# Refill order of the wide weight pieces, gate gathers one slot ahead, and five weight positions in a mixture-of-experts kernel

## The chip, the cores and the metric

The kernel runs on one core of a Trainium2 chip. The metric is the device time of one execution in microseconds; of several executions the median is given. A profiled execution has a time of its own and a span, which goes from its first to its last instruction.

## The reference

Two stages. The first is causal attention over 4 batches, 8 heads, 576 tokens of width 64, blended per head with a linear memory; its output, reshaped to 2304 tokens of width 512, is `x`. The second sends every token to one of 8 experts:

```python
logits = x @ w_gate
e_idx = np.argmax(logits, axis=1)
gate_w = probs[np.arange(N), e_idx]
eom = 1.0 / (1.0 + np.exp(-(x @ w_output_gate)))
for e in range(E):
    mask = e_idx == e
    if not mask.any():
        continue
    h = np.maximum(x[mask] @ w1[e], 0.0)
    ye = h @ w2[e]
    out[mask] = gate_w[mask, None] * eom[mask, e, None] * ye
```

`w1[e]` is 512 x 1024 and `w2[e]` 1024 x 512, both float32, so one expert's weights are 4 MB.

## The kernel before

The attention stage takes roughly the first 205 us and is not touched. Behind it, tokens are sorted by expert into blocks of up to 128 rows of one expert, called slots. One slot's work is done early for the expert with the most tokens (the "star" functions); 17 main slots (`NMAIN`) follow in a fixed loop; and remainders of experts that would fill only a small part of a slot are collected into two group tiles: four experts' remainders of up to 32 rows, then two of up to 64 rows.

**A main slot.** `gather(s)` fetches the 128 rows of `x` by an indirect DMA on POOL, `gather_gate(s)` the 128 gate factors by another. `stage_x` transposes the rows on PE (L1376), copies them out on ACT twice, as `xh` rounded and as `x32` full (L1381, L1383), and POOL takes the difference `xl` (L1384). `gemm1` is 24 products (L1405): each weight is split into a high part `whi` and a low part `wlo`, and the product is the sum of whi·xh, whi·xl and wlo·xh. ACT applies the ReLU (L1418). `stage_h` transposes the result (L1431), ACT copies it (`hT`, `hh`, L1434 and L1435) and POOL forms `hl` (L1436). `gemm2` is 24 more products, ACT scales the result by the gate factor (`y`, L1443) and POOL scatters it (`scatter`, L1459). The loop runs `gemm1` of slot s+1, then `stage_x` of slot s+2, then `gemm2` of slot s, with `stage_h` of slot s+1 in its middle.

**Expert weights.** The experts of the main slots stand in an order of "positions": position 0 is the star expert, and `NPOS` positions are loaded. `fetch` (L377, DMAs on SP, 512 KB each) fills four buffers `kept`, and `high`, `low`, `ready` (L1097 to L1104) split a piece on DVE: 0.7 us for a cast and 1.2 us for a subtraction, eight pieces to an expert. Only two positions fit into `whi` and `wlo`, so `load_expert(e)` (L1335) makes DVE wait, by `sem_1` and `sem_2`, until the slots of position e-2 have used its half. Before a slot PE waits on `sem_w` until its own position is split.

**Wide pieces.** The group tiles need weights of several experts at once. They run in 24 units, two to a slot in slots 2 to 13: unit (s, 0) before `gemm2(s)`, unit (s, 1) behind it (`plan`, `point`, `unit`, L1562). A unit reads one of two 1 MB buffers `wide`, which alternate. `wide_load(u)` (L1521) fills one with 2 or 4 DMAs issued by ACT, and PE waits on a semaphore for all of them (L1565). `refill(s, half)` (L1624) issues the load that uses the buffer that unit (s, half) has freed; it is read one slot later. ACT runs its instructions in the order in which they are written.

**Around slot 0.** `gather_gate(s)` for slots 0 to 3 and `star_out`, the scatter of the early slot, stand in a row on POOL; later gates are gathered by `gather(s + 4)`. `group_rows` (L1323) computes the rows of the group tiles. A scratch tile `hhs` (L1255) shares its memory (tag `hh`) with the tile `hh` of slot 0, and the star's result `ye` (L1358) shares the tag `xc` with the gathered rows of a group.

**The end.** Behind the loop every engine reads the number of slots and jumps over a branch (L1708, L1709) that would run 18 further slots one at a time; SP then waits for the last scatter.

The functions that are touched, with their lines:

Of the kernel before, what the change touches and what calls it, by code (L numbers as in the profile page):

```python
# [10 lines left out]
F32 = mybir.dt.float32  # L11
# [9 lines left out]
P = 128  # L21
# [3 lines left out]
DM = H * D  # L25
E = 8
F = 1024
# [5 lines left out]
KC = DG + P  # L33
QK = KC + S
NMAIN = 17
NPOS = 6
NREST = 18
NSLOT = NMAIN + NREST
NEND = E + 1
QUARTERS = 4  # L40
# [92 lines left out]
def attn_moe(ctx: ExitStack, tc: tile.TileContext, qk, vd, mz, mt, rz, beta, wgo, w1, w2, out):  # L133
# [49 lines left out]
    ze = {}  # L183
# [193 lines left out]
    def fetch(e, c):  # L377
        n = 8 * e + c
        if len(kept) < 4:
            kept.append(raw_tile(f"kept{n}"))  # L380
        raw = raws[e, c] = kept[n % 4]
        if c == 0:
            fetching["e"] = SY.value_load(order[0:1, e:e + 1], min_val=0, max_val=E - 1)
        send(raw, fetching["e"], c)
# [645 lines left out]
    def star_out():  # L1030
        V.scalar_tensor_tensor(jc, stars, 65536.0, jc, op0=ALU.mult, op1=ALU.add)
# [151 lines left out]
    def rows(i):  # L1183
        V.tensor_scalar(rowi[i], pps[i], float(MID), 0.0, op0=ALU.add, op1=ALU.add)
# [9 lines left out]
    def take():  # L1194
        d, ok, qc, qn, qt, hc, hn, ht, qr = (t8[n] for n in ("d", "ok", "qc", "qn", "qt", "hc", "hn", "ht", "qr"))
        V.scalar_tensor_tensor(d, sizes, -BIG, fin["nps"], op0=ALU.add, op1=ALU.subtract)
        V.scalar_tensor_tensor(qn, sizes, BIG, star, op0=ALU.is_le, op1=ALU.mult)
        V.scalar_tensor_tensor(ok, d, 64.0, qn, op0=ALU.is_lt, op1=ALU.subtract)
        V.tensor_scalar(ok, ok, 0.0, 0.0, op0=ALU.max, op1=ALU.add)
        V.scalar_tensor_tensor(qc, d, 32.0, ok, op0=ALU.is_gt, op1=ALU.mult)  # L1200
        V.scalar_tensor_tensor(hc, d, 0.0, ok, op0=ALU.is_gt, op1=ALU.mult)
        V.tensor_tensor_scan(qn, qc, nothing, 0.0, ALU.add, ALU.add)
        V.scalar_tensor_tensor(qt, qn, QUARTERS + 0.5, qc, op0=ALU.is_lt, op1=ALU.mult)
        V.tensor_tensor(hc, hc, qt, op=ALU.subtract)
        V.tensor_tensor(qr, qn, qt, op=ALU.mult)
        V.tensor_tensor_scan(hn, hc, nothing, 0.0, ALU.add, ALU.add)
        V.scalar_tensor_tensor(qt, d, 64.0, qt, op0=ALU.is_gt, op1=ALU.add)
        V.scalar_tensor_tensor(ht, hn, HALVES + 0.5, hc, op0=ALU.is_lt, op1=ALU.mult)
        V.tensor_tensor(qt, qt, ht, op=ALU.add)
        V.scalar_tensor_tensor(hn, hn, float(QUARTERS), ht, op0=ALU.add, op1=ALU.mult)  # L1210
        V.tensor_tensor(qc, qt, star, op=ALU.mult)
        V.tensor_tensor(taken[:, 1:], qt, rest8, op=ALU.mult)
        V.reduce_sum(taken[:, 0:1], qc, axis=AX.X)
        V.scalar_tensor_tensor(top, taken, -float(P), top, op0=ALU.mult, op1=ALU.add)
        V.tensor_tensor(group_of, qr, hn, op=ALU.add)
        V.tensor_tensor_scan(enp[:, 1:], top, back, 0.0, ALU.add, ALU.add)
# [12 lines left out]
    def hits():  # L1229
        V.tensor_single_scalar(hit[0], sl.unsqueeze(2), 0.0, op=ALU.is_equal)  # L1230
        place(0)
        star_gemm1(1, range(3, 4))
        star_relu(1)
        star_h(0)
        take()
        rows(0)
        virtual(1, 4, vs[:, 1:4], some, adj)
        hits_of(1)
        skips(0)
        for c in range(2):  # L1240
            low(0, c)
            ready()
        star_gemm2(range(2))
        place(1)
        star_h(1)
# [6 lines left out]
    mk = fin["mk"] = ctx.enter_context(tc.tile_pool(name="mk", bufs=1, side="right"))  # L1252
    pm = fin["pm"] = ctx.enter_context(tc.tile_pool(name="pm", bufs=1, space=PSUM))
    cp = ctx.enter_context(tc.tile_pool(name="cp", bufs=1, side="right"))
    hhs = mk.tile([P, F], F32, name="hhs", tag="hh")  # L1255
    more = hhs[:, :(NREST + 7) * NEND].rearrange("p (s e) -> p s e", e=NEND)
    fin["gs3"] = hhs[:, 768:768 + P]
    some = more[:, :NREST]
    t8 = dict(zip(("d", "ok", "qc"), (more[:, NREST + i, :E] for i in range(3))))
    es, adj = (more[:, NREST + 3 + 2 * i:NREST + 5 + 2 * i].rearrange("p a e -> p (a e)") for i in range(2))  # L1260
# [62 lines left out]
    def group_rows():  # L1323
        pg = pa.tile([P, 2], F32, name="pg", tag="c0")
        for g in range(QUARTERS):
            T.matmul(pg[32 * g:32 * g + 32, 0:1], ident[:, 0:32], gcol[:, g:g + 1], start=True, stop=True, tile_position=(0, 32 * g))
        for g in range(HALVES):
            T.matmul(pg[64 * g:64 * g + 64, 1:2], ident[:, 0:64], gcol[:, QUARTERS + g:QUARTERS + g + 1], start=True, stop=True, tile_position=(0, 64 * g))
        V.tensor_scalar(group_row, pg, float(MID), 0.0, op0=ALU.add, op1=ALU.add)
        skipped(group_skip, pg)  # L1330
        V.tensor_tensor(group_out, group_row, group_skip, op=ALU.subtract)
# [21 lines left out]
    def gather_gate(s):  # L1353
        g = st[s]["g"] = mk.tile([P, 1], F32, name=f"g{s}", tag="g", bufs=4)
        G.indirect_dma_start(out=g, out_offset=None, in_=gd[:MID if s == "e" else NT + 1], in_offset=bass.IndirectOffsetOnAxis(ap=slot_rows(s), axis=0))

    def star_y():
        ze["y"] = mk.tile([P, DM], F32, name="ye", tag="xc")  # L1358
        A.activation(ze["y"], ze["py"], AF.Copy, scale=st["e"]["g"])

    def star_out():
# [52 lines left out]
    def gemm1(s, mid=None):  # L1414
        h = pa.tile([P, F], F32, name=f"h{s}", tag="h")
        gemm(s, [h[:, :512], h[:, 512:]], st[s]["x1"], 0, 2, mid)
        h32 = st[s]["h"] = bq.tile([P, F], F32, name=f"h32_{s}", tag="h32")
        A.activation(h32, h, AF.Relu)  # L1418
        done(s, sem_1)
# [44 lines left out]
    def split(e, c, eng):  # L1464
        high(e, c, eng)
        low(e, c)
        ready()
# [24 lines left out]
    star_gemm2(range(6, 8))  # L1492
    high(0, 7, A)
    star_y()
    for c in range(4, 6):
        low(0, c)
        ready()
# [19 lines left out]
    def numbers(g0, g1):  # L1517
        for g in range(g0, g1):
            cst["e", g] = A.value_load(groupi[0:1, g:g + 1], min_val=0, max_val=E - 1)

    def wide_load(u):  # L1521
        b = u % 2
        if b not in wide:
            wide[b] = (se if b else cp).tile([P, 2 * F], F32, name=f"wide{b}", tag=f"w{b}")
        kind, part, k = loads[u]
        ng, g0 = (QUARTERS, 0) if kind == 0 else (HALVES, QUARTERS)
        for g in range(ng):
            to = wide[b].rearrange("p (g f) -> p g f", g=ng)[:, g]
            e = ds(cst["e", g0 + g], 1)
            if kind == 0 and part == 0:  # L1530
                i = A.dma_start(to, w1[e, k // 2 * P:(k // 2 + 1) * P, k % 2 * 512:k % 2 * 512 + 512].rearrange("a p f -> (a p) f"))
            elif kind == 0:
                i = A.dma_start(to, w2[e, k * P:(k + 1) * P, :].rearrange("a p f -> (a p) f"))
            elif part == 0:
                i = A.dma_start(to, w1[e, k * P:(k + 1) * P, :].rearrange("a p f -> (a p) f"))
            else:
                i = A.dma_start(to.rearrange("p (a d) -> p a d", a=2), w2[e, k * 256:(k + 1) * 256, :].rearrange("e (a p) d -> p (e a) d", p=P))
            i.then_inc(sem_c[b], 16)
            apart(i, begun[-1:])
            begun.append(i.ins)  # L1540
            tc.no_tile_sem_insts.add(i.ins.name)
            tc.add_to_no_dep_group("wide", i.ins)
            landed[b] += 16
        loads[u] = (kind, part, k, landed[b])
# [79 lines left out]
    def refill(s, half):  # L1624
        if (s, half) in plan and ahead[0] < len(loads) and s >= 2:
            wide_load(ahead[0])
            ahead[0] += 1

    def first_h():
        place(2)  # L1630
        stage_h(0)

    gemm1(1, first_h)
    for s in range(4):
        gather_gate(s)
    star_out()
    later_slots()
    group_rows()
    numbers(0, QUARTERS)
    wide_load(0)  # L1640
    for c in range(8):
        fetch(1, c)
        split(1, c, V)
    for s in range(NMAIN):
        if 0 < s < NMAIN - 1:
            gemm1(s + 1, plan.get((s + 1, "mid")))
        refill(s - 1, 1)
        if s + 2 < NMAIN:
            stage_x(s + 2)
            regs(s + 2)  # L1650
        if s == NMAIN - 1:
            finish(s)
            break
        i = point(s, 0)
        gemm2(s, lambda: stage_h(s + 1))
        refill(s, 0)
        i = point(s, 1) or i
        if s == 13:
            tc.declare_fence(i.ins, group="wide")
        if s % 4 == 3:  # L1660
            G.drain()
        if s + 4 < NMAIN:
            gather(s + 4)
        scatter(s)
        if s in (0, 7):
            group_gather(s // 7)
        if s == 0:
            wide_load(1)
        if s == 8:
            numbers(QUARTERS, GROUPS)  # L1670
        if s < NPOS - 2:
            load_expert(s + 2)
# [101 lines left out]
```

## Time and profile before

| | us |
|---|---|
| median of 3 runs | 522.44 |
| lowest and highest run | 519.12, 524.5 |
| profiled execution, its own time | 521.64 |
| span of the profiled execution | 519.9 |
| mean granted TensorE clock of that execution | 0.968 of full |
| PE busy (matrix products) | 477.1 |

How it is read: the span is cut into stretches, and for each the profile gives the busy time of every engine, the granted clock of PE and what the DMA engines moved. Waits are listed by who waited and who released them. The chain is the line of work that ended last, followed back from the last instruction. PE's products overlap and their ends are modelled, so the distance between starts says more than the busy time.

### The profile page before, as it was taken

The numbers are of one execution on the slowest core, as the hardware profiler recorded it, in microseconds if no ns is written. First come the engines' busy times: TensorE is split into PE (matmuls) and PEld (weight loads), VectorE is DVE, ScalarE is ACT, GpSimd is POOL, SyncE is SP. The second block draws the span as 40 slices with busy tenths as digits, with TensorE's granted clock in tenths as the row PEclk, the third lists the DMA queues.
The fourth block names the chain that finished last, engine by engine and source line by source line (L and its number), as shares of the span: only waits on it lengthen the run. The fifth ranks groups of instructions, "written<-read, shape, count | busy, mean of one in ns | idle before, by whom it ended". The sixth has DMA issues, their size and how long they took to land.

```text
span 519.9 us, 10539 instructions
## 1 busy us (share of the span) xinstructions
PE 477.1 (92%) x3315; PEld 353.1 (68%) x3315; DVE 293.7 (56%) x863; ACT 262.4 (50%) x621; POOL 268.1 (52%) x264
## 2 busy tenths in 40 slices
PE   7999999999999999897799797996977899999993
PEld 4778778777777876475577474664754666666883
DVE  4988989889799878887907060042188000000445
ACT  5989988988787764354132231333230322423340
POOL 8646565666347526526865254235276335442452
PEclk8999999999999999999799997999897999999997
DMA  7442345251413611617945576268299745334241
GB/s 250 149 148 107 128 136 180 91 177 41 139 45 98 198 54 56 195 46 254 361 149 165 205 241 247 81 234 283 77 345 348 238 154 203 114 120 173 74 143 39
DMA packets 35881, 84.30 MB, mean 162 GB/s; under 512 B 4948, under 2 KB 5480, under 8 KB 35818
## 3 DMA queue, kind: packets, MB, share of 16 engines
q1 hardware_dynamic: 19274, 48.24, 27.6%
q10 hardware_dynamic: 12688, 25.30, 14.7%
q0 software_dynamic: 3856, 9.98, 5.5%
q8 instruction: 32, 0.52, 0.4%
q14 instruction: 31, 0.25, 0.1%
HBM read 74.05 MB, written 9.97 MB: 162 GB/s over the span
## 4 chain that ended last, share of the span: by engine, by line
PE 70%; DMA 12%; DVE 8%; ACT 3%; ACTq 3%; issue 2%; POOL 1%; DVEq 0%; POOLq 0%
PE py L1405 12%; PE h L1405 12%; DMA wide<-in_w 10%; PE po L675 9%; PE pt L640 7%; PE s L565 7%; PE me L731 4%; DVE wlo L1101 3%; PE sd L552 3%; PE cy L1583 2%; PE ch L1583 2%; PE hp L1431 2%; PE pt L609 2%; PE pv L794 1%; DMA xc<-xs,group_row 1%
## 5 line engine op out<-in xcount | busy, mean ns | idle before, releaser
L1098 DVE CAST whi<-kept 128x1024 fp32r<-128x1024 f32 x40 | 34.9, 872 | 183.5 <-ACTq L1412 176.4
L1436 POOL TENSOR_TENSOR hl<-hT,hh 128x512 fp32r<-128x512 f32 x32 | 44.8, 1425 | 64.2 <-ACT hh L1435 64.2
L628 ACT ACTIVATE st<-st,nm 128x128 f32<-128x128 f32 (+3 forms) x128 | 71.4, 562 | 5.5 <-DVE nm L623 4.8
L623 DVE CUSTOM_DVE_ANT_0 st<-s,mask 128x128 f32<-128x128 f32 (+3 forms) x128 | 58.3, 483 | 10.7 <-PE s L565 6.7
L1405 PE MATMUL h<-whi,xl 128*128 (+1 forms) x136 | 55.6, 409 | 4.9 <-POOL xl L1384 4.9
L1418 ACT ACTIVATE h<-h 128x1024 f32<-128x1024 f32 x17 | 17.5, 1027 | 83.0 <-PE h L1405 77.5
L1405 PE MATMUL h<-whi,xh 128*128 (+1 forms) x136 | 58.2, 428 | 0.0
L1101 DVE TENSOR_TENSOR wlo<-kept,whi 128x1024 fp32r<-128x1024 f32 x40 | 56.7, 1417 | 1.4
L1405 PE MATMUL h<-wlo,xh 128*128 (+1 forms) x136 | 55.1, 405 | 0.0
L460 POOL TENSOR_TENSOR lo<-qk,hi 128x1216 fp32r<-128x1216 f32 x15 | 42.2, 2811 | 24.5 <-ACT hi L456 19.1
L1405 PE MATMUL py<-whi,hh 128*128 (+1 forms) x128 | 54.1, 422 | 0.6 <-ACT hh L1435 0.6
L1384 POOL TENSOR_TENSOR xl<-x,xh 128x512 fp32r<-128x512 f32 x17 | 23.8, 1401 | 58.6 <-ACT x L1383 45.1
L487 ACT COPY PT<-pt 128x512 f32<-128x512 f32 (+2 forms) x89 | 45.3, 523 | 15.9 <-PE pt L640 13.7
L1405 PE MATMUL py<-whi,hl 128*128 (+1 forms) x128 | 51.1, 399 | 0.0
L1405 PE MATMUL py<-wlo,hh 128*128 (+1 forms) x128 | 51.0, 399 | 0.0
L675 PE MATMUL po<-PT,v 128*64 128x320 f32 (+4 forms) x480 | 49.1, 349 | 0.8 <-ACT oT_hT L487 0.4
L640 PE MATMUL pt<-ident,st 128*128 128x128 f32 x320 | 48.1, 281 | 0.0
L675 PEld LDWEIGHTS po<-PT,v 128*64 128x64 f32 x480 | 29.6, 137 | 17.7 <-issue 2.8
L640 PEld LDWEIGHTS pt<-ident,st 128*128 128x128 f32 x320 | 35.6, 142 | 7.0 <-issue 1.9
L1434 ACT COPY hT<-hp 128x512 f32<-128x512 f32 x34 | 20.1, 591 | 38.0 <-PE hp L1431 38.0
L1405 PEld LDWEIGHTS h<-whi,xh 128*128 128x128 f32 x136 | 26.9, 198 | 16.7 <-ACT hh L1435 7.4
L1435 ACT CAST hh<-hp 128x512 fp32r<-128x512 f32 x32 | 19.0, 595 | 33.3 <-PE py L1405 31.0
(337 smaller groups left out, 1032.9 us busy)
## 6 DMA issues: line engine op xcount, KB each, us to landing
kept<-in_w SPq DMA_DIRECT2D x40, 512.0 KB
wide<-in_w ACTq DMA_DIRECT2D x64, 256.0 KB
qk<-in_qk SPq DMA_DIRECT2D x15, 640.0 KB
wide<-in_w ACTq DMA_DIRECT2D x16, 512.0 KB
v<-in_vd SPq DMA_DIRECT2D x16, 320.0 KB
xs<-xd SPq DMA_DIRECT2D x12, 256.0 KB
star<-in_w SPq DMA_DIRECT2D x6, 512.0 KB
mz<-in_mz SPq DMA_DIRECT2D x4, 324.0 KB
```

The lines of the kernel that those rows point to most:

```text
L460: G.tensor_tensor(c["lo"][:, TQ:], c["raw"][:, TQ:], f32(c["hi"])[:, TQ:], op=ALU.subtract)
L487: (A.copy if e == "ACT" else V.tensor_copy)(dst(), src())
L565: T.matmul(c()["ss", q][j], l[r, lc], m[r, KC:KC + w], start=(a == 0), stop=(a == 2))
L623: V.tensor_tensor_reduce(st[:, :w], c()["ss", qt][j], mask[:, 512 - w:512], -SCALE, 3.0e38, ALU.add, ALU.min, negm()[:, i:i + 1])
L628: A.activation(st, st, AF.Exp, bias=c()["negm"][:, i:i + 1], scale=-1.0, accum_out=sums()[:, qt, 2 * p + j:2 * p + j + 1])
L640: T.transpose(pt[:, (m * k1 + i) * P:(m * k1 + i + 1) * P], st[:, i * P:(i + 1) * P], ident)
L675: T.matmul(po[64 * j:64 * j + 64, qs - q0:q1 - q0], vt[:, k, 64 * j:64 * j + 64], PT[:, j, k, qs:q1], start=(k == 0), stop=(k == kn - 1))
L1098: join((A.copy if eng is A else eng.tensor_copy)(whi[:, e % 2, c, :], raws[e, c]))
L1101: join(eng.tensor_tensor(wlo[:, e % 2, c, :], raws.pop((e, c)), f32(whi[:, e % 2, c, :]), op=ALU.subtract))
L1384: G.tensor_tensor(xl, x32, f32(xh), op=ALU.subtract)
L1405: i = T.matmul(o[n % nh], l[:, z], m[:, n * 512 + part.start:n * 512 + part.stop], start=(c == 0 and k == 0 and n < nh), stop=(c == 3 and ...
L1436: G.tensor_tensor(hl[:, z], hT[:, z], f32(hh)[:, z], op=ALU.subtract)
```

## The change

Five things. `NPOS` goes from 6 to 5. `refill(s, 0)` stands ahead of `gemm2(s)`, right behind unit (s, 0), and `refill(s, 1)` right behind unit (s, 1) instead of behind the next `gemm1`. Gates are gathered one slot ahead inside the loop, where four were gathered ahead of it and the others with `gather(s + 4)`; `star_out` moves up behind `star_y`. `numbers` (four register reads on ACT) moves ahead of `gemm1(1)`, `group_rows` into the middle of `gemm2(0)`, the first `wide_load` into slot 0 and the split of position 1 behind it. The scratch tile moves to the tag `xc` and `ye` to the tag `hl`; `rows(0)` is computed a little earlier.

```diff
-NPOS = 6
+NPOS = 5
@@ take, hits
         V.tensor_tensor(hc, hc, qt, op=ALU.subtract)
+        rows(0)
         V.tensor_tensor(qr, qn, qt, op=ALU.mult)
...
         take()
-        rows(0)
         virtual(1, 4, vs[:, 1:4], some, adj)
@@
-    hhs = mk.tile([P, F], F32, name="hhs", tag="hh")
-    more = hhs[:, :(NREST + 7) * NEND].rearrange("p (s e) -> p s e", e=NEND)
-    fin["gs3"] = hhs[:, 768:768 + P]
+    scratch = mk.tile([P, DM], F32, name="scratch", tag="xc")
+    more = scratch[:, :(NREST + 7) * NEND].rearrange("p (s e) -> p s e", e=NEND)
+    fin["gs3"] = scratch[:, 256:256 + P]
@@
     def star_y():
-        ze["y"] = mk.tile([P, DM], F32, name="ye", tag="xc")
+        ze["y"] = mk.tile([P, F], F32, name="ye", tag="hl")[:, :DM]
@@
     star_y()
+    star_out()
@@
+    numbers(0, QUARTERS)
     gemm1(1, first_h)
-    for s in range(4):
-        gather_gate(s)
-    star_out()
     later_slots()
-    group_rows()
-    numbers(0, QUARTERS)
-    wide_load(0)
-    for c in range(8):
-        fetch(1, c)
-        split(1, c, V)
     for s in range(NMAIN):
         if 0 < s < NMAIN - 1:
             gemm1(s + 1, plan.get((s + 1, "mid")))
-        refill(s - 1, 1)
         if s + 2 < NMAIN:
             stage_x(s + 2)
             regs(s + 2)
+        if s == 0:
+            gather_gate(0)
+            wide_load(0)
+        if s < NMAIN - 1:
+            gather_gate(s + 1)
...
         i = point(s, 0)
-        gemm2(s, lambda: stage_h(s + 1))
         refill(s, 0)
+        gemm2(s, lambda: (group_rows() if s == 0 else None, stage_h(s + 1)))
         i = point(s, 1) or i
+        refill(s, 1)
...
         if s + 4 < NMAIN:
-            gather(s + 4)
+            gather(s + 4, False)
         scatter(s)
         if s in (0, 7):
             group_gather(s // 7)
         if s == 0:
             wide_load(1)
+            for c in range(8):
+                fetch(1, c)
+                split(1, c, V)
```

On ACT, slots 2 and 3 before: from the copy `x_4` of slot 4 over `hT` of slot 3 and `y` of slot 2 to the first two refills (two repeated issues of each load, and the other copies, are left out at the dots).

```order
L1383 COPY x_4_4363<-px_4355 128x512
L1434 COPY hT_4408<-hp_4407 128x512
...
L1443 ACTIVATE y_4437<-py_4391,g_3889 128x512
L1531 DMA wide_3952<-in_w 128x512
...
L1418 ACTIVATE h_4_4536<-h_4508 128x1024
L1531 DMA wide_4092<-in_w 128x512
...
L1381 CAST xh_4548<-px_4543 128x512
```

The same place in the changed kernel:

```order
L1383 COPY x_4_4357<-px_4349 128x512
...
L1532 DMA wide_3964<-in_w 128x512
...
L1434 COPY hT_4408<-hp_4407 128x512
...
L1443 ACTIVATE y_4437<-py_4391,g_4203 128x512
...
L1532 DMA wide_4041<-in_w 128x512
...
L1418 ACTIVATE h_4_4534<-h_4506 128x1024
L1381 CAST xh_4542<-px_4537 128x512
```

The first refill moved from behind `y` to ahead of `hT`, the second from behind the ReLU of slot 4 (`h_4`) to ahead of it.

On POOL, around slot 0, before: from the gather of slot 3's rows (`xr`) over `hl` of slot 0 and the gates `g` to `xl` of slot 2 and `hl` of slot 1.

```order
L1367 DMA xr_3751<-xs,rowi_3513 128x512
L1436 TENSOR_TENSOR hl_3855<-hT_3853,hh_3854 128x512 x2
L1355 DMA g_3885<-gd,rowi_3512 128x1
L1355 DMA g_3887<-gd,rowi_3513 128x1
L1355 DMA g_3889<-gd,rowi_3513 128x1
L1355 DMA g_3891<-gd,rowi_3513 128x1
L1363 DMA out<-ye,rowe 2304x512
L1384 TENSOR_TENSOR xl_4008<-x_2_4010,xh_4007 128x512
L1436 TENSOR_TENSOR hl_4049<-hT_4047,hh_4048 128x512 x2
```

The same place in the changed kernel:

```order
L1367 DMA xr_3751<-xs,rowi_3513 128x512
L1363 DMA out<-ye,rowe 2304x512
L1436 TENSOR_TENSOR hl_3894<-hT_3892,hh_3893 128x512 x2
L1384 TENSOR_TENSOR xl_3939<-x_2_3941,xh_3938 128x512
L1355 DMA g_3962<-gd,rowi_3512 128x1
L1355 DMA g_3969<-gd,rowi_3513 128x1
L1436 TENSOR_TENSOR hl_4000<-hT_3998,hh_3999 128x512 x2
```

The star's scatter went ahead of `hl` of slot 0, and of the four gate gathers ahead of `xl` of slot 2 two stand behind it and two have left this place.

## Rows read from the trace of the kernel before

**Rows 1.** Windows: length, busy time per engine, PEclk, DMA share, GB/s.

```profile
238.00:266.00 28.00, 21.67 (x95) 17.25 (x96) 19.47 (x17) 8.36 (x15) 23.13 (x17) 0.88 0.93 334
...
373.00:394.50 21.50, 15.86 (x80) 10.53 (x76) 17.98 (x16) 6.27 (x11) 16.79 (x11) 0.93 0.83 296
...
413.50:430.00 16.50, 16.50 (x80) 11.15 (x77) 0.00 (x0) 5.57 (x10) 6.28 (x6) 1.00 0.49 165
```

**Rows 2.** Waits of PE from 240 to 520: total, times, longest.

```profile
PE cy L1583 <- DMA wide<-in_w: 11.9, 5, 4.6
PE ch L1583 <- DMA wide<-in_w: 7.5, 4, 3.4
...
PE chp L1594 <- ACT ch L1589: 1.1, 1, 1.1
```

**Rows 3.** Chain in order of time, 250 to 402: start, length, what.

```profile
250.41 7.57 PE h L1405 x23
...
259.34 6.24 DMA xc<-xs,group_row
...
291.43 3.01 PE py L1405 x12
...
299.10 5.69 PE h L1405 x24
...
318.73 7.71 PE h L1405 x24
...
363.97 4.55 PE py L1405 x12
...
394.59 7.38 PE h L1405 x24
```

**Rows 4.** Timeline of ACT and PE, 300 to 393: start, length, [idle before].

```profile
300.58 1.85 ACTq L1531 DMA_DIRECT2D wide<-in_w  x4
304.87 1.02 ACT L1418 ACTIVATE h<-h 128x1024 f32<-128x1024 f32 x1 [4.52 <-PE h L1405]
306.13 1.86 ACTq L1531 DMA_DIRECT2D wide<-in_w  x4
306.15 1.06 PE L1583 MATMUL ch<-wide,cx 128*32 128x512 f32 x8 [0.94 <-DMA wide<-in_w]
...
380.21 2.17 ACTq L1533 DMA_DIRECT2D wide<-in_w  x4
...
392.66 1.93 PE L1583 MATMUL cy<-wide,cx 128*32 128x512 f32 x8 [4.60 <-DMA wide<-in_w]
```

**Rows 5.** Timeline of ACT, POOL and PE around slot 0, 236 to 251.

```profile
236.42 0.59 ACT L1435 CAST hh<-hp 128x512 fp32r<-128x512 f32 x1 [2.36 <-DVE rowi L1184]
...
245.18 1.79 POOL L1355 DMA_INDIRECT g<-gd,rowi  x1 [0.30 <-issue]
...
247.27 1.78 POOL L1363 DMA_INDIRECT out<-ye,rowe  x1 [0.30 <-ACT hh L1435]
249.07 1.28 POOL L1384 TENSOR_TENSOR xl<-x,xh 128x512 fp32r<-128x512 f32 x1
...
250.41 0.80 PE L1405 MATMUL h<-whi,xl 128*128 x1 [4.91 <-POOL xl L1384]
```

**Rows 6.** Timeline of DVE and PE in the last slots, 488 to 515.

```profile
488.10 0.69 DVE L1098 CAST whi<-kept 128x1024 fp32r<-128x1024 f32 x1 [83.86 <-ACTq L1412]
...
493.58 0.39 PE L1405 MATMUL h<-whi,xh 128*128 x1
...
513.61 1.23 DVE L1101 TENSOR_TENSOR wlo<-kept,whi 128x1024 fp32r<-128x1024 f32 x1
```

**Rows 7.** Line 1709, the branch: ns min/median/max, first and last start.

```profile
L1709 POOLq INC_SWDGE_SEM  x1: 248/248/248, 515.8 to 515.8; - x1
L1709 DVEq EVENT_SEMAPHORE  x1: 21/21/21, 518.8 to 518.8; - x1
```

**Rows 8.** Line 1708, a register read on ACT: ns min/median/max.

```profile
L1708 ACTq TENSOR_LOAD <-numi x1: 281/281/281, 512.1 to 512.1; - x1
```

## The prediction

> **What bounds the kernel now.** I read the windows first. In the loop of slots PE is busy almost all the time where it waits for nothing: from 413.5 to 430 it is busy for the whole 16.5 us at clock 1.00 [rows 1]. Elsewhere there are gaps, and the waits of PE say whose they are: 11.9 us in 5 waits and 7.5 us in 4 for wide pieces that had not landed, and 1.1 us for a ReLU of a group [rows 2]. So the loop is bound by PE, and what can be won is PE's waits and what they do to its clock. The chain shows the second part: 24 products take 5.69 us at 299.10, but 7.71 at 318.73 and 7.38 at 394.59, and 12 products take 3.01 us at 291.43 but 4.55 at 363.97 [rows 3]; each of the slow ones stands behind a wait of about 3 us or more, after which the granted clock was lower (0.93 on average from 373 to 394.5) [rows 1]. The full level is 2.4 GHz, the lower one 1.2.
>
> Why the pieces are late is in the timeline. The load that unit (4, 0) reads is issued at 300.58, behind `y` of slot 3, and PE begins the unit at 306.15: 5.57 us for 1 MB, and PE had waited 0.94 of them [rows 4]. But its buffer was free at 291.43, when unit (3, 0) ended and `gemm2` of slot 3 began [rows 3]: 9.15 us were given away. The other buffer was free at 299.10, where the next `gemm1` begins, and its load is issued at 306.13, behind the ReLU at 304.87 [rows 3, 4]: 7 us. Where expert weights are fetched at the same time a load is slower: 380.21 to 392.66, 12.45 us [rows 4].
>
> Two more places. At 250.41 PE has stood still for 4.91 us for `xl` of slot 2, which POOL reached only at 249.07, behind four gate gathers and the star's scatter, up to 1.79 us each [rows 5]. And at the end DVE is the last: it splits a sixth position until 514.84 (513.61 + 1.23) [rows 6].
>
> **The change part by part.** The sum is made against the profiled execution's 521.64 us; the median of the runs is 0.8 us above it, which I do not correct for.
>
> *Refills.* Nothing is added: the same DMAs go in another order. A slot without waits lasts 14.8 us, from the unit at 290.37 (291.43 less its 1.06 us) to 305.21 (306.15 less the wait) [rows 3, 4]. The new refill (s, 0) stands on ACT behind the ReLU (1.02) and two copies of 0.59 (a row of that shape is `hh`) [rows 4, 5], so in that slot at 304.87 + 1.02 + 1.18 = 307.07; the piece is needed at 305.21 + 14.84 = 320.05: a lead of 13.0 us, against 4.6 before (300.58 to 305.21). Refill (s, 1) stands behind the last two copies and `y`, about 1.3 us behind the end of its unit: a lead of 12.5 (14.8 less the unit's 1.0 and 1.3). An undisturbed load needs 5.57 and the slowest needed 12.45, so by single loads every wait goes: 11.9 + 7.5 = 19.4 us. With the waits goes the slow clock behind them: 7.71 - 5.69 = 2.02; 7.38 - 5.69 = 1.69; 4.55 - 3.01 = 1.54; and two units at 1.93 instead of 1.06 (one at 392.66, its like ahead of 318.73), 1.74; together 7.0 us. The group's ReLU now stands ahead of refill (5, 1), which held it for 1.86 us of issuing: its 1.1 us go too.
>
> The added wait: each refill makes ACT wait for the unit's products, and behind it stand the `hT` copies or the next ReLU. The unit would end at 305.21 + 1.06 = 306.27, before ACT reaches the refill at 307.07, so the wait is nothing as long as the piece has landed. The issue itself, 1.85 us, ends at 308.92, and the copies that follow wait for transposes that stand 12 products (3.01 us) behind the unit, at 309.3 or later [rows 3, 4]. If a piece is late, ACT is late by as much as PE is, not more.
>
> What is late next: all transfers share one bandwidth. The stretch 373 to 394.5 moves 296 GB/s, 6.4 MB in 21.5 us [rows 1]; without its waits (4.60 and about 1 and the slow unit) it would last some 15 us, which asks for 424 GB/s, where the busiest window reaches 334 at a DMA share of 0.93. At 334 the 6.4 MB need 19 us, 4 more than PE would leave. The longer lead lets most of these bytes move earlier, and the position that is no longer loaded frees 2 MB just behind. Between 0 and 4.0 us I take 1.6 us of waits left, nearer to 0 because one slot's lead has to be used up first.
>
> Here a page speaks against the change. The Trainium skill, "DMA: Bandwidth & Descriptors", section "Issuing engines are not separate DMA queues", says that transfers started by different engines run on the same 16 DMA engines and interleave. By that rule a load beside one other busy queue should take about twice as long, 11.1 us (an estimate from the 5.57); the trace's 12.45 agrees in kind and is longer. Either is below the lead for one load, and neither is for two in a row.
>
> *Around slot 0.* The scatter and the gates leave the way of `xl` of slot 2: it then follows its copies directly, and PE's 4.9 us go. So does the clock drop: 23 products took 7.57 against 5.69 x 23/24 = 5.45, 2.1 us [rows 3]. `hh` of slot 0 no longer waits 2.36 us for the scratch tile's readers [rows 5]; `gemm2(0)` is then bound by PE's own `gemm1(1)`, transposes and register reads, which I put at 1.2 us earlier (between 0 and 2.36). `group_rows` keeps its products on PE. The four reads on ACT cost 4 x 0.28 = 1.1 us [rows 8], in the time in which ACT now waits for transposes; without that cover at most that 1.1. Against it: the gather of the group's rows takes 6.24 us to land [rows 3] and is reached only about 5 us earlier, because `hl` and other gathers stand ahead of it while DMA is full (0.93) [rows 1]; I take 0.7 us more of waiting, between 0 and 2. Sum: 4.9 + 2.1 + 1.2 - 0.7 = 7.5 us. The split of position 1 starts about 2 us later on DVE, and is read only from slot 4 on. `rows(0)`: between 0 and 0.5 us gained, counted as 0.
>
> *Gates in the loop.* A gather of up to 1.79 us [rows 5] now stands on POOL ahead of `hl`, where it stood behind. POOL is busy for 6.28 of 16.5 us [rows 1], and `hl` is read by `gemm2` one `gemm1` (5.69 us) later [rows 3]: 0, at worst 1.8 in a slot in which POOL is late anyway.
>
> *Five positions.* No main slot reads the sixth: PE starts the last slot's products at 493.58, while DVE is still splitting that position, which it began at 488.10 after 83.86 us of waiting [rows 6]. Its removal frees 4 MB of transfers, and the end: DVE came over the branch at 518.8, POOL was done with the last scatter at 516.05 (515.8 + 0.25) [rows 7], so 2.7 us.
>
> Sum: 521.6 - 19.4 - 7.0 - 1.1 + 1.6 - 7.5 - 2.7 = 485.5 us.
>
> **The rivals.** *Transfers collide.* The loads come earlier but the bandwidth is used up in the stretches where experts are fetched, and half of the 26.4 us of waits and slow clock stay: 485.5 - 1.6 + 13.2 = 497 us. For it: shares of 0.83 and 0.93 [rows 1]. Against: between these stretches the share is near 0.5 and the lead is more than twice an undisturbed load. Chance 0.19. The page's rule above is on this side.
>
> *The start gains nothing.* The wait for `xl` is followed by one for the group's rows or by another step on POOL, since DMA is full there: 485.5 + 7.5 = 493 us. For it: 6.24 us to land; against it: only one transfer there is on PE's way. Chance 0.08.
>
> *The fifth position is needed by the branch.* If the tokens needed a sixth position, the branch would run 18 slots, each with eight splits of at least 0.69 + 1.23 = 1.92 us on DVE [rows 6], 15.4 us a slot: 485.5 + 18 x 15.4 = 763 us or more, slower than before. It decides at the first such slot. Against it: the last slot did not wait for that position [rows 6]. Chance 0.02.
>
> **How the numbers follow.** The forecast, 485.5 us, has 0.69; its own range is 481 (no wait left, 1 us more at the start, and the runs' spread) to 490 (4 us of waits left, the start 2 short). To hold 8 in 10 the range reaches to the collision's 497 and a little over: 480 to 498. About 1% either way is what a measurement of this kernel can tell from no change. Faster by over 1%: forecast, collision and start, 0.96; within 1%: 0.02, for what I have not seen; slower: 0.02.
>
> **What would show it.** Right: PE's waits for wide pieces below 4 us in total, PE at clock 1.00 from the third slot on, no wait for `xl` at the start, the last instruction about 1 us behind POOL's last semaphore. The collision would show as waits for wide pieces while `kept` is fetched, at a DMA share above 0.9. Wrong: ACT late at `hT` or at the ReLU with PE waiting for `hl`, `xl` or `hh`; or any time in the branch.

## The result, and the profile after

The changed kernel takes 484.94 us (median of 4 runs, 484.05 to 486.0). The kernel before, run beside it, takes 522.53 (519.12 to 524.5). The ratio is 0.929, interval 0.9235 to 0.9341. The forecast was 485.5. The profiled execution took 484.58 us, its span is 482.9, 37.0 us shorter than the span before (519.9), and its mean granted clock is 0.989 (before 0.968).

The waits of PE after, from 200 us on (total, times, longest), answer to [rows 2]:

```profile
PE pc L1557 <- DMA xc<-xs,group_row: 3.9, 1, 3.9
PE px L1376 <- DVE skip L1188: 1.4, 1, 1.4
PE pye L1130 <- ACT hTe L1124: 0.7, 1, 0.7
```

Not one wait for a wide piece is left, nor the one for the group's ReLU, nor the one for `xl`. One has grown: the transposes of the group's rows, `xc`, stood 0.85 us for their gather before and stand 3.9 now.

Where the 37.0 us came from is read from equal pieces of both traces. The first is the loop, from the transposes `px` in front of unit (2, 0) to the first product of `gemm1` of slot 15, which follows the last unit. Windows of before, then of after (length, busy time per engine, PEclk, DMA share, GB/s):

```profile
271.64:481.07 209.43, 188.83 (x910) 129.93 (x908) 54.33 (x48) 63.13 (x106) 90.01 (x72) 0.96 0.59 201
```

```profile
266.63:446.53 179.90, 179.90 (x909) 126.02 (x907) 58.26 (x48) 63.11 (x106) 92.26 (x72) 1.00 0.65 221
...
296.00:308.00 12.00, 12.00 (x66) 8.33 (x65) 5.47 (x5) 4.84 (x8) 6.88 (x7) 1.00 0.95 330
...
360.00:400.00 40.00, 40.00 (x201) 28.25 (x200) 21.85 (x17) 13.59 (x23) 27.27 (x20) 1.00 0.77 273
```

The loop is 29.5 us shorter. Before, PE stood idle for 20.6 of its 209.4 us (209.43 - 188.83) and was busy for 188.8; now it is busy in every one of the 179.9 us, at clock 1.00. So 20.6 us are waits and 8.9 us (188.83 - 179.90) the same instructions at a higher clock. The start, up to that `px`, gave 5.0 us (271.64 - 266.63), and the end 2.5 (38.83 from 481.07 to 519.9 before; 36.37 from 446.53 to 482.9 now). 29.5 + 5.0 + 2.5 = 37.0.

Of the start's 5.0 us, 1.65 stand there before the changed part begins: the first product of the routing, at the end of the attention stage, starts at 199.49 before and at 197.84 after.

```profile
199.49 0.19 PE L232 MATMUL rk<-oha,upper 128*128 128x40 bf16 x1 [0.24 <-DVE oha L267]
```

```profile
197.84 0.19 PE L232 MATMUL rk<-oha,upper 128*128 128x40 bf16 x1 [0.24 <-DVE oha L267]
```

From 9 to 15 us PE's granted clock was 0.72 before and 1.00 after. Two profiles of one kernel differ there in the same way (last section), so this part is not the change's: the start itself gave 3.4 us (5.01 - 1.65).

The leads are in the timeline of ACT and PE after, as in [rows 4]:

```profile
296.25 1.02 ACT L1418 ACTIVATE h<-h 128x1024 f32<-128x1024 f32 x1 [4.52 <-PE h L1405]
297.44 0.59 ACT L1381 CAST xh<-px 128x512 fp32r<-128x512 f32 x1 [0.16 <-issue]
297.62 0.34 ACTq L1532 DMA_DIRECT2D wide<-in_w  x1
...
306.65 2.10 ACTq L1532 DMA_DIRECT2D wide<-in_w  x4
...
311.20 1.06 PE L1584 MATMUL ch<-wide,cx 128*32 128x512 f32 x8
318.79 1.06 PE L1584 MATMUL ch<-wide,cx 128*32 128x512 f32 x8
```

The load issued at 297.62 is read at 311.20, 13.6 us later (forecast 13.0), and the one issued at 306.65 at 318.79, 12.1 us later (forecast 12.5). Both are read with no idle time in front.

The chain shows what is left at the start (start, length, what):

```profile
241.92 5.46 PE h L1405 x24
...
250.80 7.21 DMA xc<-xs,group_row
258.15 1.08 PE pc L1557 x4
259.23 7.56 PE h L1405 x24
266.79 0.44 PE px L1376 x4
```

`gemm1` of slot 2 now runs at once and in 5.46 us (before, 4.91 us of waiting for `xl` and 7.57 for 23 products [rows 3, 5]). The chain then stands for 7.21 us on the gather of `xc`, issued at 250.80. PE idles for 3.94 us, up to 258.15, and from 258.15 to 266.79 its granted clock is 0.69: the transposes of `xc` take 1.08 us and the next `gemm1` 7.56. Before, the same two took 0.63 and 5.46:

```profile
265.71 0.63 PE pc L1556 x4
266.34 5.46 PE h L1405 x24
```

The slow stretch has moved by one slot.

### The profile page after: what moved, and what is told of

It reads as the page before. It is cut to its first block, busy times and chain, and to the rows that moved or that the text cites. A ratio compares the mean times of both kernels' runs of the same rounds, so it can differ in the third digit from the quotient of the medians.

```text
span 482.9 us, 10479 instructions
## 1 busy us (share of the span) xinstructions
PE 465.7 (96%) x3315; PEld 348.3 (72%) x3315; DVE 282.1 (58%) x847; ACT 262.6 (54%) x621; POOL 266.2 (55%) x264
## 4 chain that ended last, share of the span: by engine, by line
PE 88%; DVE 3%; DMA 2%; issue 2%; ACT 1%; POOL 1%; POOLq 0%; SPq 0%; DVEq 0%; ACTq 0%
PE h L1405 20%; PE py L1405 17%; PE po L675 9%; PE pt L640 8%; PE s L565 7%; PE me L731 4%; PE cy L1584 3%; PE ch L1584 3%; PE hp L1431 3%; PE sd L552 3%; PE pt L609 2%; DMA xc<-xs,group_row 1%; PE px L1376 1%; PE pv L794 1%; PE pl L899 1%
## 5 line engine op out<-in xcount | busy, mean ns | idle before, releaser
L1436 POOL TENSOR_TENSOR hl<-hT,hh 128x512 fp32r<-128x512 f32 x32 | 45.8, 1454 | 52.1 <-ACT hh L1435 52.1
L1098 DVE CAST whi<-kept 128x1024 fp32r<-128x1024 f32 x32 | 32.7, 1022 | 67.4 <-ACTq L1412 59.8
L1405 PE MATMUL h<-whi,xh 128*128 (+1 forms) x136 | 56.7, 417 | 0.0
L1405 PE MATMUL h<-whi,xl 128*128 (+1 forms) x136 | 54.0, 397 | 0.0
L1405 PE MATMUL h<-wlo,xh 128*128 (+1 forms) x136 | 53.9, 396 | 0.0
L1405 PE MATMUL py<-whi,hh 128*128 (+1 forms) x128 | 53.0, 414 | 0.0
L1405 PE MATMUL py<-whi,hl 128*128 (+1 forms) x128 | 50.0, 391 | 0.0
L1101 DVE TENSOR_TENSOR wlo<-kept,whi 128x1024 fp32r<-128x1024 f32 x32 | 45.1, 1411 | 1.1
```

Of the source, the lines that this page charges most:

```text
L1098: join((A.copy if eng is A else eng.tensor_copy)(whi[:, e % 2, c, :], raws[e, c]))
L1101: join(eng.tensor_tensor(wlo[:, e % 2, c, :], raws.pop((e, c)), f32(whi[:, e % 2, c, :]), op=ALU.subtract))
L1405: i = T.matmul(o[n % nh], l[:, z], m[:, n * 512 + part.start:n * 512 + part.stop], start=(c == 0 and k == 0 and n < nh), stop=(c == 3 and ...
L1436: G.tensor_tensor(hl[:, z], hT[:, z], f32(hh)[:, z], op=ALU.subtract)
```

## The experiments

The changed kernel was run in one set only. What is gained or lost against its 484.94 us therefore compares different sets, in which the kernel before had medians from 518.89 to 522.53 us.

**Both refills late again.** In the changed kernel:

```
+        refill(s - 1, 1)       # behind gemm1(s + 1)
...
-        refill(s, 0)           # ahead of gemm2(s)
         gemm2(s, ...)
+        refill(s, 0)
         i = point(s, 1) or i
-        refill(s, 1)
```

> The changed kernel with both refills put back to where they stood before (the first half's behind gemm2, the second's behind gemm1 of the next turn but one); start, gates and five positions stay changed. Theory of the prediction (a wide piece arrives late only because its transfer is issued late): the waits of TensorE for wide come back in slots 1 to 15, some 19 us, and the clock falls in them as before, some 8 us more, so about 512 us (506 to 516). Rival (the waits went because the sixth position's 4 MB no longer cross the gathers and the pieces): few waits for wide come back, below 495 us.

Measured: 504.85 us (504.24 to 510.75, 5 runs), ratio to before 0.971 (0.9636 to 0.9784). The waits in its profile, which is that of the 510.75 us execution:

```profile
PE ch L1584 <- DMA wide<-in_w: 10.1, 5, 4.0
PE cy L1584 <- DMA wide<-in_w: 7.5, 4, 3.7
PE pc L1557 <- DMA xc<-xs,group_row: 4.4, 1, 4.4
...
PE chp L1595 <- ACT ch L1590: 1.1, 1, 1.1
```

The waits are back, 17.6 us with the ReLU's 1.1 behind them, though five positions are loaded and 4 MB less are moved. The time lies just below the range given. Since the five executions differ by 6 us, the same kernel was taken once more:

> The kernel with both refills late once more, for a second profile: the first was of its slowest execution (510.75 us, median 504.85). Theory (what its executions differ by is the clock in and behind the waits, not the waits): waits for wide of 17 to 18 us again, and a granted clock of 0.98 and above with about 505 us. Rival (the waits themselves differ): a profile at 505 us with waits for wide of 12 us or less.

Measured: 509.49 us (505.86 to 511.65, 4 runs), ratio 0.987 (0.973 to 1.0003), profile at 510.23 us and a granted clock of 0.975:

```profile
PE ch L1584 <- DMA wide<-in_w: 8.5, 4, 3.8
PE cy L1584 <- DMA wide<-in_w: 6.7, 5, 2.5
```

15.2 us of waits. This profile too is of an execution at 510 us, so whether one at 505 us waits less or only loses less clock was not settled. Late refills cost 20 to 25 us in the changed kernel by the two sets.

**The refills alone, on the kernel before.** The two calls move as in the change and nothing else does.

> The kernel before with the early refills alone; the old start, four gates ahead and six positions stay. Theory: the loop's waits go, 28 us, so about 494 us (490 to 499), and what is left to 485 is the start (5 us) and the end (2.5 us). Rival (early refills need the bandwidth that the other edits free): waits for wide of more than 5 us stay in the trace and the time is above 500 us.

Measured: 491.19 us (490.82 to 492.5), ratio 0.9445 (0.9374 to 0.9516), 28.5 us less than the 519.73 beside it. The waits from 230 us on:

```profile
PE h L1405 <- POOL xl L1384: 4.2, 1, 4.2
PE pc L1556 <- DMA xc<-xs,group_row: 0.5, 1, 0.5
PE py L1405 <- ACT h L1418: 0.5, 1, 0.5
```

The wide pieces are on time with six positions and four gates ahead too. The rival, that they need the bandwidth that the other parts free, falls.

**Six positions in the changed kernel** (`NPOS = 6`).

> The changed kernel with six positions loaded in place of five. Theory: only the end grows, by DVE's casts of the sixth position, 2.5 us, so 487.4 us (486 to 489), without a wait for wide. Rival (the sixth position's transfers make the wide pieces late again): waits for wide of 1 us and more in the last slots and 490 us or more. Second rival (it is free): 485 us.

Measured: 486.66 us (484.03 to 488.66, 6 runs), ratio 0.9357 (0.93 to 0.9414): 1.7 us over the changed kernel, within the spread of the two sets. PE's only wait from 230 us on is the 3.9 us for `xc`. The chain, though, ends on DVE again, behind the last `y`:

```profile
470.95 0.69 ACT y L1443
471.64 0.04 ACTq L1412
...
471.78 0.70 DVE whi L1098
```

So the position costs its splits at the end and no wait.

**The old start, with early refills and five positions.**

> The kernel before with early refills and five positions; the start alone stays as it was (gates four ahead, group rows and the star's output ahead of the loop). Theory: what the start brought is missing, 5.0 us by the two traces, so 490 us (488 to 493), with the wait for xl of 4.9 us back in front of gemm1 of slot 2. Rival (the start only moves the wait from xl to the group rows' xc and brings nothing): 485 us.

Measured: 489.89 us (489.23 to 490.41, 6 runs), ratio 0.942 (0.9367 to 0.9474): 4.95 us over the changed kernel, without overlap of the runs.

```profile
PE h L1405 <- POOL xl L1384: 4.9, 1, 4.9
```

Beside the early refills the start is worth about 5 us by the runs, and not the forecast's 7.5. By the two traces the `px` in front of unit (2, 0) starts 4.25 us later (270.88 against 266.63), but 1.29 of these stand at the end of the attention stage already (199.13 against 197.84), so in these traces the start's own share is nearer to 3. Which of its edits brings what was not tried.

**The group's rows first.** In the changed kernel:

```
         if s % 4 == 3:
             G.drain()
+        if s in (0, 7):
+            group_gather(s // 7)
         if s + 4 < NMAIN:
             gather(s + 4, False)
         scatter(s)
-        if s in (0, 7):
-            group_gather(s // 7)
```

> The changed kernel with the gather of the group's rows (xc) issued on POOL ahead of the gather of rows 4 and the scatter of slot 0, some 4.3 us earlier (246.5 in place of 250.8 us). Theory: xc lands about 253.7 us, when TensorE wants it (258.15 less a wait of 3.94), so the wait goes, and with it the fall of the clock in gemm1 of slot 3 (7.56 us in place of 5.67): 3.9 + 1.9 = 5.8 us, about 479 us (478 to 481). Rival (the transfers of expert 1 and the first wide pieces hold it up wherever it is issued): a wait of 2 us and more stays, 483 to 485 us.

Measured: 479.82 us (478.21 to 482.88, 6 runs), ratio 0.9242; no run as slow as the fastest of the changed kernel (484.05). The chain around the place, of the execution at 478.6 us and clock 0.999, and POOL's issue of the gather:

```profile
242.22 5.44 PE h L1405 x24
...
254.63 0.44 PE pc L1557 x4
255.06 5.47 PE h L1405 x24
```

```profile
245.74 1.25 POOL L1549 DMA_INDIRECT xc<-xs,group_row  x1
```

The gather is issued 5.1 us earlier than in the changed kernel. PE never waits from 230 us to the end, and `gemm1` of slot 3 takes 5.47 us. 5.1 us come back of the 5.8 expected, by medians of two sets. This version beats both kernels by its times; the intervals of the two ratios (0.9191 to 0.9294, and 0.9235 to 0.9341 for the change) overlap.

**The group's transposes later as well.** The run before, with

```
-    plan[1, 1] = [lambda: group_turn(0)]
+    plan[3, "mid"] = lambda: group_turn(0)
```

> As the run before, and the transposes of xc stand in the middle of gemm1 of slot 3 in place of ahead of it (2.8 us later). Theory: nothing is left to wait for, so the same 479 us as the run before (478 to 481). Rival (xc lands late in the run before): up to 3 us less than that run.

Measured: 481.03 us (478.07 to 481.36, 6 runs), ratio 0.9244 (0.9195 to 0.9292), no less than the run before. `xc` is not late there any more; instead a new wait shows, 1.0 us for `xl` at the `gemm1` that now comes sooner.

**Five positions alone, on the kernel before** (`NPOS = 5`).

> The kernel before with five positions in place of six and nothing else. The run with late refills was 15 us faster than the kernel before, though start and five positions bring only 4.9 and 1.7 us beside early refills. Theory A (the sixth position's transfers are part of what makes the late pieces late): waits for wide fall from 19.4 us by 5 us or more, 508 to 513 us. Theory B (the sixth position costs its 2 us at the end only): 517 to 519 us.

Measured: 517.41 us (516.98 to 520.21, 6 runs), against 518.89 beside it, ratio 0.9966 (0.9915 to 1.0017).

```profile
PE ch L1583 <- DMA wide<-in_w: 8.5, 3, 3.8
PE cy L1583 <- DMA wide<-in_w: 7.8, 3, 3.8
```

The waits fall by 3.1 us to 16.3, the time by 1.5 and not beyond doubt. Theory A falls, and the time is that of theory B; but where the 1.5 us come from, the end or the waits, this run does not show.

**The start alone** (late refills and six positions in the changed kernel).

> The changed kernel with late refills and six positions, so that only the start (gates one ahead, group rows and the star's output in the loop) differs from the kernel before. Theory A (the sixth position makes late pieces later): the start brings its 5 us and no more, 514 to 516 us. Theory B (the start shifts the pieces' times against the gathers and takes waits for wide away): 505 to 510 us.

Measured: 511.89 us (508.94 to 520.11, 6 runs), ratio 0.9839 (0.9783 to 0.9896), 7.0 us less than the 518.89 beside it, with 16.4 us of waits for wide. It lies between the two theories, 2.1 us below A's range and 1.9 above B's, and decides for neither. The parts, each alone on the kernel before, bring 28.5 + 7.0 + 1.5 = 37.0 us, and the change 37.6 (522.53 - 484.94). So the parts add up. Start and five positions together brought 15 us in the first set with late refills and about 7, by its ratio, in the second; the 8.5 of the two alone lie between.

**One half early.** Two runs leave the refill of one half early and put the other's back.

> The changed kernel, but only the refill of a slot's first wide piece stands early; the second's goes back behind gemm1 of the next turn. Theory (each piece waits for its own late issue): the waits in front of the first halves stay away and those in front of the second halves come back, about 10 of the 17.6 us that both late refills had, so some 11 us more than the changed kernel, 496 us (492 to 500). Rival (one buffer's early pieces give the other the time that it lacks): 490 us or less.

> The changed kernel, but only the refill of a slot's second wide piece stands early; the first's goes back behind gemm2. Theory: the waits in front of the first halves come back, some 8 to 9 us, so 494 us (490 to 498), and with the run before the two losses add up to the 20 us of both late refills. Rival (the pieces share the queue, and the one that is late pushes the other): each of the two loses 15 us or more.

Measured: with the first half early 498.3 us (497.19 to 499.78), ratio 0.967 (0.9562 to 0.9779); with the second early 510.52 us (506.63 to 516.61, 10 runs), ratio 0.9877 (0.9805 to 0.9949). The losses against the changed kernel are 13.4 and 25.6 us. The first is near its 11; the second is as much as both late refills together, so neither theory has it: the halves are not worth the same.

With the first half early the second is waited for twice in all, 3.83 and 4.62 us, both times where DMA is full (shares of 0.95 from 296.5 to 308 and 0.97 from 363.5 to 375). The first of the two: the issue on ACT, the wait on PE and the window around them:

```profile
297.20 2.50 ACTq L1532 DMA_DIRECT2D wide<-in_w  x4
...
307.69 1.93 PE L1584 MATMUL ch<-wide,cx 128*32 128x512 f32 x8 [3.83 <-DMA wide<-in_w]
```

```profile
296.50:308.00 11.50, 7.67 (x44) 5.46 (x40) 3.84 (x4) 4.28 (x8) 6.33 (x6) 0.93 0.95 343
```

With the second early, the first halves are late instead. The issue on ACT and the first such wait:

```profile
278.75 4.27 ACTq L1532 DMA_DIRECT2D wide<-in_w  x8
...
287.46 1.93 PE L1584 MATMUL ch<-wide,cx 128*32 128x512 f32 x8 [4.07 <-DMA wide<-in_w]
```

Put behind `gemm2`, the first half's load stands directly ahead of the second's: eight DMAs in one row from 278.75. PE wants the first piece at 283.39 (287.46 - 4.07), 4.6 us behind its issue, and gets it 4.07 us late. The second load in the row is not the cause here: with both refills late the same piece, issued alone at 277.62, made PE wait 3.97 us. By halves, over the whole of both traces, the waits for the second pieces fall from 7.3 us (both late) to 1.7, and those for the first rise from 10.3 to 17.6. The clearest case, with both late and then with the second early:

```profile
313.42 2.14 ACTq L1532 DMA_DIRECT2D wide<-in_w  x4
...
322.47 1.07 PE L1584 MATMUL ch<-wide,cx 128*32 128x512 f32 x8
```

```profile
316.28 4.65 ACTq L1532 DMA_DIRECT2D wide<-in_w  x8
...
324.47 1.07 PE L1584 MATMUL ch<-wide,cx 128*32 128x512 f32 x8 [3.02 <-DMA wide<-in_w]
```

With both late PE had waited for the second half in between (2.82 us ahead of 313.76), and that gave the first half's load 9.05 us until it was read. With the second on time PE wants it 5.17 us behind its issue (321.45). So here a wait at one half gave the other its lead; how much the two loads in a row cost each other beside that was not taken apart. The late refill of the first half leaves 4.6 us to its unit. That of the second, left late alone, leaves 6.7 (issued at 297.20, wanted at 303.86), which is enough at a DMA share of 0.83 (282 to 290) and not at 0.95.

## Why the prediction was right

- **The mechanism holds.** Pieces were late because their load was issued late: with both refills back the waits return (17.6 and 15.2 us), with the refills alone they go, on either kernel.
- **The loop: 29.5 us against 25.9 forecast** (19.4 + 7.0 + 1.1 - 1.6). The waits are right: 20.6 us of idle time against 20.5. The clock is undersized: the forecast took five slow groups, 7.0 us, from single rows of the chain; all of PE's busy time in the loop gives 8.9. And of the 1.6 us set aside for waits that stay, none stayed.
- **Transfers do not collide.** The demand of 424 GB/s in the stretch of 15 us was right as a sum and wrong as a limit. From 296 to 308 the share is 0.95 at 330 GB/s and PE does not wait, because the pieces read there were issued 12 to 14 us before. From 360 to 400 the mean is 273 GB/s with PE busy throughout. So a lead of almost a slot was enough to spread the bytes. The Trainium skill, "DMA: Bandwidth & Descriptors", section "Issuing engines are not separate DMA queues", has the transfers of all engines interleave. The trace agrees: from 296 to 308 after, the queues of SP, ACT and POOL moved 2.10, 1.33 and 0.52 MB in the same 12 us. With the longer lead that cost PE nothing. The load of 12.45 us that the prediction set beside it had two busy queues next to it and not one: from 380 to 392.7 SP moved 2.78 and POOL 0.69 MB, and ACT 1.05.
- **The start: 5.0 us against 7.5, and only 3.4 of them the change's.** This is the term that was mis-sized, in both directions. `gemm1(2)` starts 3.6 us sooner than PE was ready for it before (241.92 against 250.41 - 4.91 = 245.50): 1.65 from the clock in the attention stage and 1.9 from the change, where 1.2 was forecast. The waiting for `xl` (4.9) and its slow clock (2.1) are gone as forecast. Against that `xc` is waited for 3.94 us and not 0.85, 3.1 more where 0.7 was forecast, and that wait brings a fall of the clock of its own: (7.56 - 5.46) + (1.08 - 0.63) = 2.5 us, for which the forecast had nothing. 1.65 + 1.9 + 4.9 + 2.1 - 3.1 - 2.5 = 4.95, the 5.0 that are found. The second rival (the wait for `xl` is followed by one for the group's rows) is thus half true, and the run with the group's rows first shows it: 5.1 us come back by the order of POOL's gathers alone.
- **The end: 2.5 us against 2.7**, and 1.7 and 1.5 by the two runs on the positions, neither clear of their spread. The branch was not needed: PE has 3315 products in both profiles, so no slot ran in it. After, DVE reads the number at 385.6 us already, before at the end.

```profile
L1709 DVEq TENSOR_LOAD <-numi x1: 312/312/312, 385.6 to 385.6; - x1
```

- **The added waits cost nothing.** PE waits nowhere in the loop for `hl`, `hh` or `h`, so neither ACT's waits for the units nor the gate gathers ahead of `hl` are on the path.

The errors were +3.6 us in the loop, -4.1 at the start and -0.2 at the end, and the attention stage added 1.65 that no term stood for. They nearly cancel: on the profiled execution the forecast gain of 36.1 us became 37.0. The mechanism was right; that the time came out within 0.6 us of the forecast was luck.

## What to carry to other kernels

Where a pool of two buffers feeds an engine that is the bound, look for the time from the buffer's last reader to the issue of its next load: that gap, and not the transfer alone, can be what a wait for DMA measures. Here closing it took all 19.4 us away without a byte less being moved (the run with the refills alone). Each refill belongs directly behind its own reader: with only the first half's there 13.4 us were lost, with only the second's 25.6. And when a step that the bound engine waits for is made faster, price the next wait with its fall of the clock, as was done for the one removed: here putting one gather ahead of two others on POOL was worth another 5 us.

## What was not expected of the hardware

What a wait costs in clock does not follow from its length alone. In the chain of before PE waited 3.37 us ahead of the unit at 290.37, and the 12 products behind it took 3.01 us, the full speed; 2.93 us ahead of the unit at 316.79 were followed by 24 products in 7.71 us [rows 3]. The prediction took the first group as its measure of full speed and set down every slow one to a wait of about 3 us, without the wait in front of the fast one. The two waits, in the timeline of before:

```profile
290.37 1.06 PE L1583 MATMUL ch<-wide,cx 128*32 128x512 f32 x8 [3.37 <-DMA wide<-in_w]
...
316.79 1.93 PE L1583 MATMUL ch<-wide,cx 128*32 128x512 f32 x8 [2.93 <-DMA wide<-in_w]
```

In the second profile with late refills a wait of 2.16 us stands ahead of 12 products of 4.54 us. Its timeline, then its chain:

```profile
358.68 1.06 PE L1584 MATMUL cy<-wide,cx 128*32 128x512 f32 x8 [2.16 <-DMA wide<-in_w]
```

```profile
359.75 4.54 PE py L1405 x12
```

The clock also falls where the change does nothing. The two profiles with late refills are of one kernel. Near the start of the attention stage PE waits 2.35 us in the first and 2.44 in the second, and then, from 9 to 15 us (first profile, second profile):

```profile
9.00:15.00 6.00, 5.89 (x57) 5.25 (x55) 5.08 (x18) 5.55 (x13) 5.89 (x3) 1.00 0.67 265
```

```profile
9.00:15.00 6.00, 6.00 (x28) 5.27 (x29) 3.38 (x10) 3.76 (x9) 5.90 (x4) 0.50 0.63 252
```

The granted clock is 1.00 in one and 0.50 in the other, and the first product of the routing starts at 197.86 and at 200.62: 2.8 us between two executions of one kernel, far from any wait of the loop. The executions with late refills differ by more (504.24 to 511.65 us in nine runs), but the version with the group's rows first, in whose profile PE waits nowhere from 230 us on, spreads over 4.7 us too (478.21 to 482.88). How much of a spread comes from the waits is therefore not shown, and a forecast of the clock term from one trace can be off by several us.
